# Attention and two expert layers on one core: two bursts of products with v per chunk instead of three, and the inverse sums spread by ScalarE

## The chip, the core and the metric

The kernel runs on one core of a Trainium2 chip. The metric is the device time of one execution in microseconds. Three executions of the kernel before took 1208.04, 1212.86 and 1212.77 us, median 1212.77. Five engines work side by side: TensorE (PE, its weight loads PEld), VectorE (DVE), ScalarE (ACT), GpSimd (POOL) and the DMA queue of SyncE (SP). They meet only at semaphores.

## The reference, cut to what matters

```python
q_rot, k_rot = rotate(q), rotate(k)              # 2 batches, 8 heads, 576 positions, 64 wide
scores = matmul(q_rot, k_rot.T) / sqrt(64)
attn = exp(scores - scores.max(-1))
attn = attn / (attn.sum(-1) + 1e-9)
x = matmul(attn, v)                              # then 1152 x 512
x = (silu(x @ w_gate) * (x @ w_val)) @ w_out     # 512 -> 1536 -> 512
P = sinkhorn(exp(x @ w_gate2 - max))             # 8 rounds, 8 experts
out = sum_e P[:, e] * (relu(x @ w1[e]) @ w2[e])  # 512 -> 1024 -> 512
```

The change is in the attention alone, in the sums, their inverses and the product with v.

## The kernel before

The 16 heads are taken as 8 pairs, numbered n = 0 to 7. A pair has nine units u = 0 to 8. Each is a tile of 128 queries by 576 keys, and unit 4 holds the last 64 queries of both heads. For a unit TensorE makes the scores `s` (L257), VectorE takes the negative row maximum `ng` (L262), ScalarE takes the exponential `p` and adds up the row sums as it goes (L278), and TensorE turns `p` around by four transposes into `t` (L297), which VectorE, or ScalarE for units 0, 2 and 6, copies to SBUF (L312, `turned`). Eight of the nine units leave 64 columns over; they are turned together (`rest`, L319 to L323) and copied into `q` by VectorE (L328).

The product with v is made per chunk. Chunk 0 covers units 0 to 3 (256 queries), chunk 1 units 4 to 8 (320 queries). Five products j = 0 to 4 (`values`, L364) add up in one PSUM tile `pv`; j = 0 to 3 read the turned `p`, j = 4 reads `q`. Each j is two matmuls, one for each head of the pair, that write the two halves of the partitions. In the trace each of these fp32 matmuls shows as two records, so a single j is four records, and one head's matmul is two.

The sums are inverted once per chunk (`inverse`): VectorE adds 1e-9 (L333), takes the reciprocal (L334), copies the four columns of it out to 64 columns each, `iv` (L336), and for chunk 1 two blocks of 64 x 64 into the tile `both` (L340). TensorE turns `iv` around and multiplies `both` by `fold` (L349, L351), ScalarE copies the outcome to `rc` (L355), and VectorE multiplies `pv` by `rc` (L373, `summed`), which gives the attention's output `xf`.

The work is set out in steps. Pair n starts at step 9n with unit 0; each step has slots in a fixed order (`SLOTS`: pe0 is the scores, act0 the exponentials, dve0 the copies of turned weights, dve1 the sums, dve2 the row maxima, pe1 the turning, pe2 the rest, pe3 the spreading and the products with v). Four tables place the chunk's work in steps after t0 = 9n + 5 (chunk 0) or 9n + 10 (chunk 1): `REST`, `SPREAD`, `VALUES` (one step for each j) and `SUMMED`.

```python
SPREAD = (0, 2)
VALUES = ((1, 1, 3, 4, 4), (1, 2, 2, 4, 4))
SUMMED = (7, 6)
```

TensorE and ScalarE are held to the slots' order within a step; VectorE's order is found by the scheduler, and then each engine runs its list strictly in order. PSUM is tight: two buffers for scores, two for `t` (turned weights and the spread sums share them) and two for `rest` and `pv`. So the scores of unit u + 2 wait for the exponential of unit u, and each third use of `t` waits for the copy of the first. GpSimd meanwhile prepares the next pairs' rotated q and k, and two half tiles of the first layer's weights are converted (L120 to L136) in the steps of pairs 2 and 3. The gated layer (`gated`) and the experts (`experts`) follow when the attention's last `xf` is there.

Of the kernel before, what the change touches and what calls it, by code (L numbers as in the profile page):

```python
# [10 lines left out]
F32 = mybir.dt.float32  # L11
F32R = mybir.dt.float32r
U32 = mybir.dt.uint32
AF = mybir.ActivationFunctionType
ALU = mybir.AluOpType
# [3 lines left out]
B, H, S, D = 2, 8, 576, 64  # L19
# [21 lines left out]
ENGINES1 = ("vvvv", "pppv")  # L41
LOAD_V = -2
REST = (1, 0)
SPREAD = (0, 2)
VALUES = ((1, 1, 3, 4, 4), (1, 2, 2, 4, 4))
SUMMED = (7, 6)
ACT_TURNS = (0, 2, 6)
CONVERSIONS = (18, 32)
WARM = 20
# [7 lines left out]
def fused(ctx, tc, qk, v, rope, wgv, wo, wg2, w1, w2, out):  # L57
    nc = tc.nc
# [94 lines left out]
    def attention(xT, W):  # L153
        with ExitStack() as st:
            inp.append(pool("inp", bufs=2, stack=st))
            ap_ = pool("att", stack=st)
# [14 lines left out]
            X, HL, ST, P, SUM, PT, PV, R, XF, RC, SC, TP = ({} for _ in range(12))  # L171
# [154 lines left out]
            def rested(n, c):  # L326
                ps = R.pop((n, c, "rest"))
                nc.vector.tensor_copy(out=parts(n, c)[1], in_=ps[:, 0:CS[c][1]])  # L328

            def inverse(n, c):  # L330

                s1 = SUM.pop((n, c))
                nc.vector.tensor_scalar(out=s1, in0=s1, scalar1=1e-9, scalar2=None, op0=ALU.add)  # L333
                nc.vector.reciprocal(out=s1, in_=s1)  # L334
                R[n, c, "inv"] = iv = ap_.tile([128, 4, D], F32, tag="iv", name="iv")
                nc.vector.tensor_copy(out=iv, in_=s1[:, 0:4].unsqueeze(2).to_broadcast([128, 4, D]))  # L336
                if c == 1:
                    for h in range(2):
                        r = slice(64 * h, 64 * h + 64)
                        nc.vector.tensor_copy(out=both[r, r], in_=s1[r, 4:5].to_broadcast([64, 64]))  # L340

            def spread(n, c, part):

# [42 lines left out]
            def at(step, slot, fn, *args):  # L386
                plan.setdefault((max(step, FIRST), SLOTS.index(slot)), []).append((fn, args))
# [5 lines left out]
            for n in range(pairs):  # L393
                b = 9 * n
                if n > 1:
                    at(max(b + LOADS[1], 2), "load", load, n, 1)
                    at(max(b + LOADS[0], 2), "load", load, n, 0)
                if n:
                    at(b + LOAD_V, "load", load_v, n)
                    t0, t1 = (b + TURNS[1], b + TURNS[0]) if n > 1 else (b + TURNS1[1], b + TURNS1[0])  # L400
                    for i, t in ((1, t0), (0, t1)):
                        w = LAG if n > 1 and i else 0

                        e0, e1, e2, e3 = ENGINES1[i] if n == 1 else "pppp" if i else "pppv"
                        for dt, e, fn, args in ((0, e0, mult, (0,)), (1 + w, e1, mult, (1,)), (2 + w, e2, add, ()),
                                                (3 + w, e3, low, ())):
                            if fn is low:
                                at(t + dt, "act1", high, n, i)
                            at(t + dt, *(("pool", fn, n, i, *args, pool_) if e == "p" else ("dve3", fn, n, i, *args, nc.vector)))
                        at(b + STACKS[i] if n > 1 else t + 3, "dma", stack, n, i, nc.sync)  # L410
                for u in range(9):
                    at(b + u, "pe0", scores, n, u)
                    at(b + u, "dve2", row_max, n, u)
                    at(b + u + 1, "act0", exps, n, u)
                    at(b + u + 2, "pe1", turn, n, u)
                    if u in ACT_TURNS:
                        at(b + u + 2, "act2", turned, n, u)
                    else:
                        at(b + u + 3, "dve0", turned, n, u)
                for c in range(2):  # L420
                    t0 = b + 5 + 5 * c
                    at(t0, "dve1", inverse, n, c)
                    at(t0 + REST[c], "pe2", rest, n, c)
                    at(t0 + REST[c] + 1, "dve1", rested, n, c)
                    at(t0 + SPREAD[c], "pe3", spread, n, c, 0)
                    at(t0 + SPREAD[c], "act3", spread, n, c, 1)
                    for j in range(5):
                        at(t0 + VALUES[c][j], "pe3", values, n, c, j)
                    last = n == pairs - 1
                    ts = t0 + SUMMED[c]  # L430
                    at(ts, "dve3", summed, n, c)
                    if last:
                        cs = slice(CS[c][0], sum(CS[c]))
                        at(ts, "pool", finish, n, 0, cs)
                        at(ts, "dma", finish, n, 1, cs, nc.vector)
                    elif c == 1:
                        at(ts + 1, "act1", finish, n, 0)
                        at(ts + 1, "pool", finish, n, 1, slice(0, S), pool_)
# [14 lines left out]
            for x in blocks:  # L453
                nc.gpsimd.memset(x.bitcast(F32), 0.0)
            both = ap_.tile([128, 128], F32, name="both")
            nc.gpsimd.memset(both, 0.0)
            fold = ap_.tile([128, 64], F32, name="fold")
            nc.gpsimd.tensor_tensor(out=fold, in0=ident[:, 0:64], in1=ident[:, 64:128], op=ALU.add)
            tab = tabs[1]
# [242 lines left out]
    xT = new_x()  # L702
    W = {}
    attention(xT, W)
    ps = pool("ps", bufs=8, space=PSUM)
    x2 = new_x()
# [59 lines left out]
```

## Time and profile before

| what | value |
|---|---|
| median of three executions | 1212.77 us |
| the profiled execution's own time | 1212.68 us |
| its span, first to last instruction | 1210.6 us |
| TensorE busy, weight loads, VectorE, ScalarE, GpSimd | 99%, 89%, 45%, 28%, 7% |
| first score product of pair 0 | 13.90 us |
| first product of the gated layer | 178.21 us |
| share of TensorE in the chain that ended last | 94% |

The span is cut into an attention of about 164 us and dense layers of about 1030 us, in which TensorE works without a break. A busy share over the whole span says little about the attention; the pairs have to be read one by one. A pair is cut here at the first score product of its unit 0.

### The profile page before, as it was taken

The page shows a single profiled execution, that of the slowest core. Times are in us where ns is not written, and L with a number is a line of the kernel's source. Part 1 is how long each engine was busy: PE and PEld are TensorE (multiplying, and loading weights), DVE is VectorE, ACT ScalarE, POOL GpSimd, SP SyncE. Part 2 cuts the span into 40 slices and gives each one's busy share as a digit, 9 for nine tenths or more (in the row PEclk, how much of TensorE's full clock was granted, in tenths as well). Part 3 has the DMA queues.
Part 4 walks back from the last instruction along what each step waited for, and adds up shares of the span by engine and source line. Part 5 has one row for each costly group of instructions (what it writes and reads, how often), then busy time and mean ns, then how long its engine had stood idle before and what let it go on. Part 6 is the DMA issues. An engine that isn't in the chain of part 4 may idle for free.

```text
span 1210.6 us, 15264 instructions
## 1 busy us (share of the span) xinstructions
PE 1193.5 (99%) x6456; PEld 1074.7 (89%) x6456; DVE 542.0 (45%) x850; ACT 334.7 (28%) x599; POOL 90.5 (7%) x86
## 2 busy tenths in 40 slices
PE   7999999999999999999999999999999999999998
PEld 6666669999999999899899999989989989998997
DVE  7699868998742453232232332332323233233221
ACT  4556544443411412121131221212202112122110
POOL 5468400000000000000000000000000000000000
PEclk7899999999999999999999999999999999999999
DMA  4767503332211301010120220210102012020001
GB/s 158 207 163 187 144 25 116 120 125 87 88 53 57 135 1 53 30 58 19 52 70 1 70 70 1 70 68 3 49 22 70 15 56 70 1 70 1 9 18 52
DMA packets 24115, 80.52 MB, mean 67 GB/s; under 512 B 4272, under 2 KB 4784, under 8 KB 21872
## 3 DMA queue, kind: packets, MB, share of 16 engines
q1 hardware_dynamic: 24048, 79.56, 21.2%
q8 instruction: 50, 0.82, 0.3%
q14 instruction: 17, 0.14, 0.0%
HBM read 64.80 MB, written 2.36 MB: 55 GB/s over the span
## 4 chain that ended last, share of the span: by engine, by line
PE 94%; DVE 4%; DMA 1%; ACT 1%; issue 0%; SPq 0%; DVEq 0%; ACTq 0%
PE p L148 11%; PE p L150 11%; PE p L149 11%; PE p L603 11%; PE p L604 11%; PE p L602 11%; PE s L257 4%; PE pv L364 3%; PE t L297 2%; PE po L150 2%; PE po L149 2%; PE po L148 2%; PE pg L150 2%; PE pg L148 2%; PE pv L150 2%; PE pg L149 2%
## 5 line engine op out<-in xcount | busy, mean ns | idle before, releaser
L148 PE MATMUL p<-xh,wh 128*128 128x384 f32 x768 | 257.7, 336 | 0.0
L150 PE MATMUL p<-xh,wl 128*128 128x384 f32 x768 | 256.8, 334 | 0.0
L149 PE MATMUL p<-xl,wh 128*128 128x384 f32 x768 | 256.7, 334 | 0.0
L604 PE MATMUL p<-wh,hl 128*128 128x512 f32 x576 | 224.4, 390 | 0.0
L603 PE MATMUL p<-wl,hh 128*128 128x512 f32 x576 | 224.4, 390 | 0.0
L602 PE MATMUL p<-wh,hh 128*128 128x512 f32 x576 | 224.0, 389 | 0.0
L591 ACT ACTIVATE hh<-p 128x384 fp32r<-128x384 f32 x192 | 94.2, 491 | 370.6 <-PE p L150 370.6
L592 DVE SCALAR_TENSOR_TENSOR hl<-p,hh 128x384 fp32r<-128x384 f32 x192 | 106.8, 556 | 188.7 <-ACT hh L591 188.6
L609 DVE SCALAR_TENSOR_TENSOR acc<-p,Pm,acc 128x512 f32<-128x512 f32 x63 | 47.3, 750 | 254.1 <-PE p L604 254.1
L148 PEld LDWEIGHTS p<-xh,wh 128*128 128x128 f32 x768 | 144.2, 188 | 0.9
L149 PEld LDWEIGHTS p<-xl,wh 128*128 128x128 f32 x768 | 144.2, 188 | 0.6
L150 PEld LDWEIGHTS p<-xh,wl 128*128 128x128 f32 x768 | 144.1, 188 | 0.0
L99 ACT CAST wh<-raw 128x1024 fp32r<-128x1024 f32 x64 | 67.2, 1053 | 249.3 <-PE p L604 197.7
L604 PEld LDWEIGHTS p<-wh,hl 128*128 128x128 f32 x576 | 108.1, 188 | 22.5
L603 PEld LDWEIGHTS p<-wl,hh 128*128 128x128 f32 x576 | 108.1, 188 | 22.2
L602 PEld LDWEIGHTS p<-wh,hh 128*128 128x128 f32 x576 | 108.1, 188 | 22.1
L66 DVE TENSOR_TENSOR wl<-raw,wh 128x1024 fp32r<-128x1024 f32 x64 | 78.2, 1224 | 78.4 <-ACT wh L99 76.5
L262 DVE TENSOR_REDUCE ng<-s 128x1 f32<-128x576 f32 x72 | 53.5, 749 | 15.6 <-PE s L257 10.6
L278 ACT ACTIVATE p<-s,ng 128x576 f32<-128x576 f32 x64 | 47.6, 743 | 40.1 <-DVE ng L262 39.8
L148 PE MATMUL pg<-xh,wh 128*128 128x384 f32 x144 | 48.9, 339 | 3.1 <-ACT wh L129 2.4
L149 PE MATMUL pg<-xl,wh 128*128 128x384 f32 x144 | 48.5, 337 | 0.0
L150 PE MATMUL pg<-xh,wl 128*128 128x384 f32 x144 | 48.5, 337 | 0.0
(126 smaller groups left out, 1400.6 us busy)
## 6 DMA issues: line engine op xcount, KB each, us to landing
raw<-in_w SPq DMA_DIRECT2D x64, 512.0 KB, 3.9
raw<-in_wgv SPq DMA_DIRECT2D x11, 1024.0 KB, 4.9
x<-in_qk SPq DMA_DIRECT2D x15, 576.0 KB, 4.6
raw<-in_wo SPq DMA_DIRECT2D x6, 1024.0 KB, 4.9
x<-hl SPq DMA_DIRECT2D x42, 144.0 KB, 3.4
x<-hl SPq DMA_DIRECT2D x14, 288.0 KB, 3.3
v<-in_v SPq DMA_DIRECT2D x8, 320.0 KB, 5.0
out<-acc SPq DMA_DIRECT2D x9, 256.0 KB, 2.0
```

The lines of the kernel that those rows point to most:

```text
L66: (eng or nc.vector).tensor_tensor(out=out_, in0=a, in1=hi.bitcast(F32), op=ALU.subtract)
L99: nc.scalar.copy(out=hi, in_=raw)
L148: nc.tensor.matmul(ps, wh[wsl], xh[xsl], start=first, stop=False)
L149: nc.tensor.matmul(ps, wh[wsl], xl[xsl], start=False, stop=False)
L150: nc.tensor.matmul(ps, wl[wsl], xh[xsl], start=False, stop=last)
L257: nc.tensor.matmul(ps[:, c, o:o + ks.stop - ks.start], q, k, start=t == 0, stop=t == len(terms) - 1)
L262: nc.vector.tensor_reduce(out=R[n, u], in_=SC[n, u][:, :, 0:288], axis=AX.XY, op=ALU.max, negate=True)
L591: nc.scalar.activation(out=hh[:, f], in_=po, func=AF.Relu)
L592: nc.vector.scalar_tensor_tensor(out=hl[:, f], in0=po, scalar=0.0, in1=hh[:, f].bitcast(F32), op0=ALU.max, op1=ALU.subtract)
L602: nc.tensor.matmul(po, hh[:, f, tl], wh[:, ws], start=f == 0, stop=False)
L603: nc.tensor.matmul(po, hh[:, f, tl], wl[:, ws], start=False, stop=False)
L604: nc.tensor.matmul(po, hl[:, f, tl], wh[:, ws], start=False, stop=f == KF2 - 1)
```

## The change: what it does

```diff
-SPREAD = (0, 2)
-VALUES = ((1, 1, 3, 4, 4), (1, 2, 2, 4, 4))
-SUMMED = (7, 6)
+SPREAD = (1, 2)
+VALUES = ((2, 2, 4, 4, 4), (2, 2, 4, 4, 4))
+SUMMED = (5, 5)
...
+            def guard(n, c):
+                s1 = SUM[n, c]
+                nc.scalar.activation(out=s1, in_=s1, func=AF.Copy, bias=1e-9)
+
             def inverse(n, c):
 
+                s1 = SUM[n, c]
+                nc.vector.reciprocal(out=s1, in_=s1)
+
+            def along(n, c):
+
                 s1 = SUM.pop((n, c))
-                nc.vector.tensor_scalar(out=s1, in0=s1, scalar1=1e-9, scalar2=None, op0=ALU.add)
-                nc.vector.reciprocal(out=s1, in_=s1)
                 R[n, c, "inv"] = iv = ap_.tile([128, 4, D], F32, tag="iv", name="iv")
-                nc.vector.tensor_copy(out=iv, in_=s1[:, 0:4].unsqueeze(2).to_broadcast([128, 4, D]))
+                nc.scalar.copy(out=iv, in_=s1[:, 0:4].unsqueeze(2).to_broadcast([128, 4, D]))
                 if c == 1:
-                    for h in range(2):
-                        r = slice(64 * h, 64 * h + 64)
-                        nc.vector.tensor_copy(out=both[r, r], in_=s1[r, 4:5].to_broadcast([64, 64]))
+                    nc.scalar.activation(out=both, in_=mask, func=AF.Copy, scale=s1[:, 4:5])
...
+                    at(t0 - 1, "act1", guard, n, c)
                     at(t0, "dve1", inverse, n, c)
+                    at(t0, "act2", along, n, c)
...
-            nc.gpsimd.memset(both, 0.0)
+            mask = ap_.tile([128, 128], F32, name="mask")
+            nc.gpsimd.memset(mask, 0.0)
+            for h in range(2):
+                nc.gpsimd.memset(mask[64 * h:64 * h + 64, 64 * h:64 * h + 64], 1.0)
```

Each chunk's products with v stand in two steps instead of three: j = 0 and 1 at t0 + 2, the other three at t0 + 4. The multiplication by `rc` is two steps (chunk 0) or one step (chunk 1) earlier in the plan. VectorE keeps the reciprocal alone; ScalarE adds the 1e-9, copies `iv`, and fills `both` in one instruction from a mask of ones in its two diagonal blocks. `mask` is set once at the start, on GpSimd.

The first place is on TensorE, where chunk 1 of pair 5 begins, during units 2 and 3 of pair 6 (`pv` the products with v, `t` what is turned or spread; the numbers behind names are buffers). Before:

```order
L257 MATMUL s<-x_1505,x_1644 128x288 x4
L297 MATMUL t<-ident,p 128x128 x4
L364 MATMUL pv<-p_1722,v 64x320
L257 MATMUL s<-x_1508,x_1648 128x288 x4
L364 MATMUL pv<-p_1722,v 64x320
L297 MATMUL t<-ident,p 128x128 x4
L349 MATMUL t<-ident,iv 128x128 x2
L351 MATMUL t<-fold,both 128x64
L364 MATMUL pv<-p_1722,v 64x320 x4
```

And now, the same place:

```order
L257 MATMUL s<-x_1502,x_1641 128x288 x4
L297 MATMUL t<-ident,p 128x128 x4
L257 MATMUL s<-x_1505,x_1645 128x288 x4
L297 MATMUL t<-ident,p 128x128 x4
L354 MATMUL t<-ident,iv 128x128 x2
L356 MATMUL t<-fold,both 128x64
L369 MATMUL pv<-p_1716,v 64x320 x4
```

Before, the first j of this chunk stood as two single matmuls, one head on each side of a score product; now two whole j stand together behind the spread sums, and the step ahead of them has no product with v at all. The list before has such a divided j in chunk 1 of pairs 0, 1, 2, 4, 5 and 7, which five times is a place in the pair after it (pairs 1, 2, 3, 5 and 6); the changed list has none.

The second place is on TensorE, units 6 to 8 of pair 5, where chunk 0's first products are. Before:

```order
L257 MATMUL s<-x_1242,x_1388 128x288 x4
L297 MATMUL t<-ident,pL 128x128 x4
L321 MATMUL rest<-ident,p 128x128 x2
L257 MATMUL s<-x_1239,x_1384 128x288 x4
L364 MATMUL pv<-p_1591,v 64x256 x4
L297 MATMUL t<-ident,p 128x128 x4
L257 MATMUL s<-x_1242,x_1388 128x288 x4
L297 MATMUL t<-ident,p 128x128 x4
```

And now:

```order
L257 MATMUL s<-x_1240,x_1386 128x288 x4
L297 MATMUL t<-ident,pL 128x128 x4
L321 MATMUL rest<-ident,p 128x128 x2
L354 MATMUL t<-ident,iv 128x128 x2
L257 MATMUL s<-x_1237,x_1382 128x288 x4
L297 MATMUL t<-ident,p 128x128 x4
L369 MATMUL pv<-p_1588,v 64x256 x4
L257 MATMUL s<-x_1240,x_1386 128x288 x4
L297 MATMUL t<-ident,p 128x128 x4
```

The spreading of `iv` for chunk 0 has come down behind `rest`; the two transposing groups of units 4 and 5 now stand nearer to each other, with one score product between them and the products with v behind the second; and the lone j = 2 of the step after is gone.

The third place is on ScalarE, from unit 6 of pair 4 to unit 2 of pair 5 (`p_1464` before is `p_1459` now, the turned weights of chunk 1). Before:

```order
L312 COPY p_1464<-t 128x4x128
L278 ACTIVATE p,sum<-s,ng 128x576 x3
L312 COPY p_1591<-t 128x4x128
L278 ACTIVATE p,sum<-s,ng 128x576
L209 CAST hl_1524<-x 128x576
L278 ACTIVATE p,sum<-s,ng 128x576
L355 COPY rc<-t 128x320
```

And now:

```order
L312 COPY p_1459<-t 128x4x128
L278 ACTIVATE p,sum<-s,ng 128x576
L332 ACTIVATE sum<-sum 128x5
L278 ACTIVATE p,sum<-s,ng 128x576
L343 COPY iv<-sum 128x256
L345 ACTIVATE both<-mask,sum 128x128
L278 ACTIVATE p,sum<-s,ng 128x576
L312 COPY p_1588<-t 128x4x128
L209 CAST hl_1522<-x 128x576
L278 ACTIVATE p,sum<-s,ng 128x576
L360 COPY rc<-t 128x320
```

The addition to the sum stands behind the last exponential of chunk 1, and `iv` and `both` between the exponentials of the next pair's units 0 and 1.

## Rows read from the trace of the kernel before

**Rows 1.** Windows from pair to pair; per engine busy us (instructions), PE clock, DMA share, GB/s.

```profile
13.90:40.53 26.63, 25.59 (x110) 19.57 (x110) 17.38 (x27) 10.74 (x25) 13.24 (x12) 0.55 0.63 170
40.53:58.79 18.26, 18.26 (x129) 12.81 (x127) 14.75 (x28) 11.38 (x27) 8.13 (x8) 1.00 0.68 184
58.79:78.83 20.04, 18.81 (x129) 12.82 (x127) 19.06 (x33) 11.41 (x28) 12.82 (x11) 1.00 0.60 158
78.83:98.59 19.76, 18.64 (x129) 12.77 (x127) 18.42 (x33) 11.60 (x28) 14.32 (x13) 1.00 0.72 199
98.59:116.02 17.43, 17.43 (x127) 12.63 (x127) 15.43 (x31) 12.20 (x28) 12.68 (x11) 1.00 0.69 182
116.02:134.81 18.79, 18.29 (x128) 12.77 (x126) 15.88 (x28) 11.80 (x28) 13.71 (x12) 1.00 0.60 153
134.81:153.06 18.25, 18.25 (x128) 12.80 (x126) 14.93 (x28) 10.55 (x26) 4.63 (x6) 1.00 0.45 108
153.06:178.21 25.15, 24.47 (x173) 16.19 (x171) 17.04 (x38) 11.93 (x30) 2.34 (x2) 1.00 0.00 1
```

**Rows 2.** Chain that ended last, window 58.79 to 78.83, its shares by line.

```profile
by line: DVE ng L262 26.5%; DVE p L312 15.4%; DVE sum L333 13.6%; DVE raw L132 7.7%; issue 4.8%; ACT p L278 4.1%; DVE hl L66 3.8%; PE s L257 3.7%; DVE q L328 3.6%; DVE xf L373 3.6%; DVE cv L126 3.0%; ACT xh L379 2.8%; DVE cv L123 1.7%; DVE 
```

**Rows 3.** Timeline of TensorE, pair 6: start, us, engine, line, operation, tiles, count.

```profile
139.70 0.75 PE L364 MATMUL pv<-p,v 128*64 128x320 f32 x2
140.38 0.79 PE L257 MATMUL s<-x,x 128*128 128x288 f32 x4
```

**Rows 4.** Timeline of TensorE, pair 4.

```profile
102.97 0.60 PE L297 MATMUL t<-ident,p 128*128 128x128 f32 x4
103.51 0.76 PE L364 MATMUL pv<-p,v 128*64 128x320 f32 x4
104.19 0.80 PE L257 MATMUL s<-x,x 128*128 128x288 f32 x4
104.83 0.60 PE L297 MATMUL t<-ident,p 128*128 128x128 f32 x4
105.27 0.38 PE L349 MATMUL t<-ident,iv 128*128 128x128 f32 x2
...
105.75 1.30 PE L364 MATMUL pv<-p,v 128*64 128x320 f32 x8
106.98 1.06 PE L257 MATMUL s<-hl,bd 128*128 128x288 f32 x6
```

**Rows 5.** Groups by line, 13.90 to 178.21: busy us, mean ns, idle before.

```profile
L312 DVE COPY p<-t 128x512 f32<-128x512 f32 x48 | 32.8, 683 | 6.4 <-PE t L297 6.2
...
L278 ACT ACTIVATION_READ_ACCUMULATOR p<-s,ng 128x1 f32 x64 | 12.5, 196 | 0.0
...
L333 DVE TENSOR_SCALAR sum<-sum 128x4 f32<-128x4 f32 (+1 forms) x16 | 8.8, 549 | 1.9 <-ACT p L278 1.9
...
L355 ACT COPY rc<-t 128x256 f32<-128x256 f32 (+1 forms) x16 | 6.4, 399 | 9.7 <-PE t L349 4.8 <-PE t L351 4.7
...
L336 DVE COPY iv<-sum 128x256 f32<-128x256 f32 x16 | 6.2, 386 | 0.4
...
L340 DVE COPY both<-sum 64x64 f32<-64x64 f32 x16 | 5.4, 337 | 0.1
...
L123 DVE TENSOR_SCALAR cv<-cv 128x512 uint32<-128x512 uint32 x2 | 2.3, 1170 | 0.0
```

**Rows 6.** Timeline of GpSimd and VectorE at 60.9.

```profile
60.94 1.42 POOL L203 TENSOR_TENSOR x<-x 128x576 f32<-128x576 f32 x1
60.96 1.43 DVE L333 TENSOR_SCALAR sum<-sum 128x5 f32<-128x5 f32 x1
```

**Rows 7.** Timeline of all engines at 100.9.

```profile
100.92 0.81 PE L257 MATMUL s<-x,x 128*128 128x288 f32 x4
...
101.76 0.76 DVE L262 TENSOR_REDUCE ng<-s 128x1 f32<-128x576 f32 x1 [0.17 <-PE s L257]
...
102.55 0.74 ACT L278 ACTIVATE p<-s,ng 128x576 f32<-128x576 f32 x1 [0.58 <-DVE ng L262]
```

## Prediction

> **What bounds the kernel now.** I first cut the trace at the first score product of each pair and read the windows from pair to pair [rows 1]. From pair 1 on the granted clock is 1.00 (2.4 GHz), and the pairs still take different times: 18.26, 20.04, 19.76, 17.43, 18.79 and 18.25 us for pairs 1 to 6. In pairs 1, 4 and 6 TensorE is busy for the whole window: it bounds them. In pairs 2 and 3 it is not (18.81 of 20.04, 18.64 of 19.76), VectorE is at 19.06 and 18.42 us, and the chain of waits of pair 2 is almost all VectorE, with 13.6% in L333, an addition to five numbers per partition [rows 2]. Pair 5 lies between. Pair 0 runs at half clock (0.55 in the mean). Everything after 178.21 us is dense TensorE work that the change doesn't touch; it starts when the last `xf` is there. So what the attention saves should come off the end, us for us.
>
> Why do two pairs that TensorE bounds differ by 0.82 us (18.25 for pair 6, 17.43 for pair 4)? The timeline of TensorE tells. In pair 6 chunk 1's first j is divided: one head's matmul takes 0.68 us to the next score product, and the other head's stands behind that [rows 3]. In pair 4 both heads' matmuls together take 0.68 us [rows 4]: they run side by side, and a divided j pays for it twice. The division is in pairs 1, 2, 3, 5 and 6, as the order before has it, and not in pair 4.
>
> **The change, part by part.** The sum is against the profiled execution, 1212.68 us, which is 0.09 under the median of 1212.77.
>
> *The divided products.* The new order has none. In pairs 1, 5 and 6 that is 3 x 0.82 = 2.5 us. In pairs 2 and 3, which VectorE sets, it is counted below with the rest.
>
> *One burst less per chunk.* What a burst costs by itself: a single j took 0.68 us from start to start, two j together 1.23, so a second burst costs 2 x 0.68 - 1.23 = 0.13; turning four blocks took 0.54 us to the next start when a burst follows and 0.44 when other 128-wide work follows, 0.10 more [rows 4]. That is 0.23 us, and two chunks make 0.46 us a pair: a pair that TensorE bounds would fall from 17.43 to 16.97.
>
> *What then comes late.* The saved time is taken from two short steps, units 1 and 2, which now have no products at all, and there other waits are close. From the start of a score product to its row maximum it is 0.84 us, another 0.79 to the exponential, 0.74 for that [rows 7]; the scores two units on need its buffer, some 0.1 later, so two steps can't be shorter than about 2.5 us. Unit 1 stays as it was: unit 2's scores began 0.64 us, a score product's time to the next start, ahead of the turning at 102.97 [rows 4], so at 102.33, 1.41 after unit 1's. Unit 2 is now a score product and a turning, 0.64 + 0.44 = 1.08. Together 2.49: the limit is just reached. And unit 5's turning now stands one score product behind unit 4's instead of behind the products as well. It needs the `t` buffer of unit 4, which VectorE frees with a copy of 0.68 us [rows 5] that comes after unit 6's row maximum: 0.84 + 0.75 + 0.68 = 2.3 us after unit 6's scores began. TensorE needs two score products (1.28), a turning (0.44) and, by the 0.48 that `iv` and `fold` take in pair 4 [rows 4], under 0.5 for `rest` and `iv`: 2.1 to 2.2. I give back 0.25 us a pair for both (bounds: 0, and all 0.46). So 17.2 us for a pair bound by TensorE. Pairs 1, 4, 5 and 6 sum to 72.73 before and 68.8 after: -3.9 us, the divided products and 0.54 us of VectorE's lag in pair 5 among it.
>
> *VectorE's relief.* L333, L336 and L340 go: 8.8 + 6.2 + 5.4 = 20.4 us over 8 pairs, 2.5 us a pair [rows 5], far more than such small operations need, since they wait for GpSimd: the L333 at 60.96 lasts 1.43 us, and ends with GpSimd's L203 that began just before it [rows 6]. Where TensorE bounds, this is worth nothing by itself. In pairs 2 and 3 it takes VectorE from 19.06 and 18.42 to about 16.5 and 15.9 us, below TensorE's 17.2. All of it would give 2 x 17.2, that is 5.4 us; but both pairs carry a conversion, five operations of which L123 takes 1.17 us [rows 5], and these come in one cluster between units 2 and 6, where unit 3's copy and the `t` buffers wait behind them. From 17.2 (all waits gone) to 19.9 (none gone) I take 18.5 for each, about the middle, as VectorE's saving is real but the cluster stays: 39.80 to 37.0, -2.8 us.
>
> *ScalarE's new work.* The trace has none of its three operations. The addition lies between nothing and 0.4 us; the nearest row is the accumulator's read, 0.20 on one column. `iv` is 256 wide, as half the `rc` copies are, mean 0.40 [rows 5]. For `both`, 128 wide with a scale per partition, I take 0.3; the lower end is the 0.20 of a one-column read, the upper the 1.43 of the longest L333, if ScalarE too had to wait for GpSimd. Per pair 2 x (0.20 + 0.40) + 0.3 = 1.5 us, on an engine with 10.6 to 12.2 us busy of 17 to 18. It stands idle before the exponentials, 0.58 us for one, waiting for a row maximum [rows 7]. The reciprocal that `iv` needs stands on VectorE ahead of that same row maximum, so the wait for it ends first. I cost it at nothing; if that cover is gone it costs up to 1.5 us a pair.
> The Trainium skill's page "SBUF — State Buffer" (SBUF: two separate sides) says that VectorE and GpSimd share a pair of ports as an exclusive lock and that ScalarE never waits on anyone. The trace agrees on VectorE (1.43 us, to the end of L203); by the rule the upper end of 1.43 us for `both` falls away and the 0.3 stays; no run so far shows it.
>
> *The ends.* Pair 0 loses one burst behind its unit 8 (0.23 at full clock, twice that at half): -0.4. Pair 7 and the tail lose two bursts and a divided j that partly lay under a copy: -0.5.
>
> Sum: -3.9 - 2.8 - 0.4 - 0.5 = -7.6, so 1212.7 - 7.6 = 1205 us.
>
> **Rivals.**
> 1. *The short steps eat the bursts, and the conversions' cluster keeps pairs 2 and 3.* For it: the 2.49 against 2.5 us above, and 0.1 to 0.2 us lacking at unit 5; VectorE's order is strict, so a lag of one operation reaches the next `t` buffer. Against: pair 4 runs without a wait while VectorE has 15.43 us. Then only the divided products are won, 3 x 0.82 in pairs 1, 5, 6 and some 0.8 each in 2 and 3, 4.1 us with nothing at the ends: 1208.6.
> 2. *VectorE's relief counts in full.* Pairs 2 and 3 at 17.2 (-5.4 instead of -2.8) and half of the 0.25 given back (4 x 0.12): 1205 - 2.6 - 0.5 = 1202.
> 3. *The clock rises later.* The first window's mean clock of 0.55 [rows 1] means 1.2 GHz for some 24 of its 26.6 us, with TensorE busy for 25.59 of them, and 2.4 GHz from about 38 us on. The way of `iv` now crosses ScalarE; if TensorE has to stop for it in that window and the half speed lasts half as long again, 12 us, these do 6 us less work: 1205 + 6 = 1211, no change. Against: at half clock TensorE is the slow one, and the other engines are ahead of it.
> 4. *Slower: ScalarE stands in its own way.* It runs strictly in order. If `iv` waits for a reciprocal that VectorE reaches late, the next unit's exponential waits behind it, then the scores two units on, then all of TensorE. Price: the added 1.5 us a pair on the path, 8 x 1.5 = 12, less the 5 us of the divided products with the tail's: 1212.7 + 7 = 1219.7. It decides from the point where the wait and the 0.7 us of `iv` and `both` outlast ScalarE's idle time ahead of the next exponential, which is 0.58 us in the place of [rows 7]. Against: the reciprocal comes first in VectorE's order, and ScalarE idles in each pair for 5 to 8 us [rows 1].
> [...]
>
> That the change doesn't do what it says is ruled out for the bursts by the order; it can be true of the relief, if VectorE's next operation waits for GpSimd in place of the removed one. That is within case 1.
>
> **How the numbers follow.** Chances: the forecast (1203.5 to 1207.5) 0.48; rival 1 (1207.5 to 1210) 0.20; rival 2 (under 1203.5) 0.20; rival 3 0.06; rival 4 and anything else slower 0.06. About 0.5%, 6.1 us, is what a measurement of this kernel can tell from no change; its three executions lie 0.4% apart. Faster is so under 1206.6. Rival 2 lies there whole, and of the forecast's four microseconds the lower three, some 0.8 of it: 0.8 x 0.48 + 0.20 = 0.58. Slower is 0.06, and no change the rest, 0.36. The range for 8 in 10 holds the forecast and most of rivals 1 and 2: 1200 to 1210.
>
> **What would show it.** Right: windows of about 17.2 us for pairs 1, 4, 5, 6, equal among themselves; no two-record product of v around a score product; L333 and L340 gone from the chain; pairs 2 and 3 at 18 to 19 us with VectorE still near full; ScalarE's idle time before exponentials shorter by about 1.5 us a pair. The turning of unit 5 would show a short wait for a copy by VectorE. Wrong: waits of TensorE for the exponentials behind `iv`; pair 4 above 17.43; a clock of 0.5 beyond 40 us; or the attention shorter and the gated layer's first wait for weights longer by as much.

## The result and the profile after

Six executions of the changed kernel took 1199.15 to 1200.43 us, median 1199.96. Six of the kernel before took 1206.41 to 1212.86, median 1207.94. The ratio is 0.9916, with a 95% interval of 0.9894 to 0.9938: faster by 8.0 us. I had forecast 1205.0 with a range from 1200 to 1210, so the time came out at the lower edge, 0.04 us outside. The forecast gain of 7.6 us was close. What failed is the level from which it was subtracted, and that is mainly the clock in pair 0, as the rest shows.

The profiled execution took 1199.97 us, span 1198.2. Its windows from pair to pair, with the columns of [rows 1]:

```profile
13.96:34.59 20.63, 19.19 (x107) 15.58 (x107) 15.96 (x25) 10.67 (x26) 11.69 (x11) 0.72 0.53 135
34.59:51.76 17.17, 17.13 (x129) 12.80 (x127) 12.46 (x23) 12.23 (x31) 9.17 (x10) 1.00 1.00 285
51.76:70.36 18.60, 17.58 (x129) 12.77 (x128) 16.56 (x28) 13.11 (x33) 12.71 (x11) 1.00 0.65 181
70.36:89.23 18.87, 17.40 (x130) 12.83 (x128) 16.61 (x27) 12.93 (x33) 13.49 (x12) 1.00 0.72 203
89.23:106.46 17.23, 17.18 (x126) 12.79 (x127) 13.23 (x24) 12.63 (x32) 14.77 (x14) 1.00 0.70 192
...
140.87:165.42 24.55, 23.84 (x178) 16.69 (x176) 16.02 (x29) 14.31 (x38) 1.42 (x2) 1.00 0.00 1
```

Pairs 1, 4, 5 and 6 now take 17.2 us each (17.17, 17.23, 17.19 and 17.22), equal among themselves; together 68.8 us, the sum that was forecast. Pairs 2 and 3 together fell from 39.80 to 37.47, pair 7 by 0.60. The large difference is in the first row: pair 0 fell from 26.63 to 20.63, with a mean clock of 0.72 instead of 0.55. The stretch after the attention is nearly the same, 1032.8 us against 1032.4. Of the 12.7 us between the two profiled executions, 6.0 lie in pair 0 and 6.8 in pairs 1 to 7.

The chain of waits in pair 2 (51.76 to 70.36), its shares by line:

```profile
by line: DVE ng L262 14.6%; issue 12.7%; DMA x<-hl 10.3%; DVE p L312 9.7%; SPq L237 8.7%; POOL hl L66 7.6%; DVE cv L122 6.6%; PE pv L369 5.5%; PE t L297 4.7%; DVE hl L66 4.0%; PE s L257 3.9%; DVE cv L126 3.5%; DVE raw L132 3.2%; DVE xf L378
```

The addition to the sums, 13.6% in [rows 2], is gone, and what remains of VectorE there is mostly row maxima, copies and the conversion (L122, L126, L132); the first 5 us of the chain now run through the next pair's operands (POOL hl L66, SPq L237, DMA x<-hl). The groups from 13.96 to 165.42 that answer to [rows 5] (line, engine, operation, count, busy us, mean ns, idle before):

```profile
L343 ACT COPY iv<-sum 128x256 f32<-128x256 f32 x16 | 6.4, 398 | 0.3 <-DVE sum L337 0.3
...
L332 ACT ACTIVATE sum<-sum 128x4 f32<-128x4 f32 (+1 forms) x16 | 3.3, 208 | 0.4
L345 ACT ACTIVATE both<-mask,sum 128x128 f32<-128x128 f32 x8 | 3.2, 401 | 0.0
...
L123 DVE TENSOR_SCALAR cv<-cv 128x512 uint32<-128x512 uint32 x2 | 3.0, 1524 | 0.1
```

ScalarE's three operations take 0.21, 0.40 and 0.40 us, where VectorE's took 0.55, 0.39 and twice 0.34 on average, and up to 1.43 for one. The conversion's L123 has grown from 1.17 to 1.52.

The place of [rows 3, 4], TensorE in pair 6 after the change (start, us, line, operation, tiles, records):

```profile
126.39 0.80 PE L257 MATMUL s<-x,x 128*128 128x288 f32 x4
...
128.91 0.81 PE L257 MATMUL s<-x,x 128*128 128x288 f32 x4
129.55 0.60 PE L297 MATMUL t<-ident,p 128*128 128x128 f32 x4
...
130.50 1.30 PE L369 MATMUL pv<-p,v 128*64 128x320 f32 x8
131.72 1.06 PE L257 MATMUL s<-hl,bd 128*128 128x288 f32 x6
```

No half j stands around a score product any more; the eight records of two j take 1.22 us to the next start. Units 1 and 3 start 2.52 us apart, at the limit of 2.5 that the prediction worked out, and TensorE has no wait there.

### The profile page after: what moved, and what is told of

The parts are those of the page before. It is cut to its first block, busy times and chain, and to the rows that moved or that the text cites. A ratio compares the mean times of both kernels' runs of the same rounds, so it can differ in the third digit from the quotient of the medians.

```text
span 1198.2 us, 15270 instructions
## 1 busy us (share of the span) xinstructions
PE 1179.4 (98%) x6456; PEld 1070.6 (89%) x6456; DVE 525.5 (44%) x802; ACT 342.7 (29%) x639; POOL 89.9 (8%) x88
## 4 chain that ended last, share of the span: by engine, by line
PE 93%; DVE 3%; DMA 1%; issue 1%; ACT 1%; SPq 0%; POOL 0%; DVEq 0%; POOLq 0%
PE p L148 11%; PE p L150 11%; PE p L149 11%; PE p L614 11%; PE p L613 11%; PE p L612 11%; PE s L257 3%; PE pv L369 3%; PE t L297 2%; PE po L150 2%; PE po L149 2%; PE po L148 2%; PE pg L150 2%; PE pg L148 2%; PE pv L150 2%; PE pg L149 2%
## 5 line engine op out<-in xcount | busy, mean ns | idle before, releaser
L66 DVE TENSOR_TENSOR wl<-raw,wh 128x1024 fp32r<-128x1024 f32 x64 | 78.1, 1223 | 78.4 <-ACT wh L99 76.5
L262 DVE TENSOR_REDUCE ng<-s 128x1 f32<-128x576 f32 x72 | 54.0, 753 | 19.2 <-PE s L257 17.2
```

What stands on the lines that cost most here:

```text
L66: (eng or nc.vector).tensor_tensor(out=out_, in0=a, in1=hi.bitcast(F32), op=ALU.subtract)
L262: nc.vector.tensor_reduce(out=R[n, u], in_=SC[n, u][:, :, 0:288], axis=AX.XY, op=ALU.max, negate=True)
```

## Experiments

Theory A throughout: in pairs 1 to 7 the change works as forecast, and what differed is when TensorE's clock rises in pair 0, which is not of the change's making. Theory B: the change itself shortened pair 0, or one of its parts is worth something other than I said.

### The same kernels again

`e1_before_again` is the kernel before, unchanged, and `e5_after_again` the changed one, unchanged.

> The kernel before, unchanged, to see its executions one by one. Theory A (the clock's rise in pair 0 varies from execution to execution, whatever the kernel): the executions fall into two groups about 5 us apart, near 1207.5 and near 1212.5, and a profile of the faster kind has pair 0 at about 21 us with the clock up near 25 us, pairs 1 to 6 as in the profile shown (18.3, 20.0, 19.8, 17.4, 18.8, 18.3 within 0.3). Theory B (the change brings the earlier rise): every execution near 1212.5, or, if faster, with the clock still rising near 38 us.

Measured: 1211.54 us median of 12 executions, 1205.51 to 1213.08, ratio to the others beside it 0.9998 (0.9976 to 1.0020). Five executions were at 1205.5 to 1207.8 and seven at 1210.8 to 1213.1. The profile fell on the slower kind: the clock rose at 38.55 us, and pair 0 took 28.04. So the kernel before was not seen in a trace with an early rise; that it has one is read from its mean clocks below.

> The changed kernel once more, beside many executions of before on the same chip, for the clock in pair 0. Theory A (when the clock rises to 2.4 GHz in pair 0 is left to the execution): its executions spread as those of before do, over some 5 us, from about 1199 to 1205, and beside an equal clock the gain is 6.5 to 8 us. Theory B (the change itself brings the early rise): all executions stay within 1199 to 1200.5.

Measured: 1200.99 median of 12, 1197.87 to 1208.50, ratio 0.9937 (0.9913 to 0.9961). Both kernels spread over some 10 us, in groups by the mean clock of the execution. Put side by side at an equal clock (90 executions of the kernel before that ran beside the experiments, 18 of the changed one; the table has the clocks that both show):

| mean granted clock | before, mean us (count) | after, mean us (count) | difference |
|---|---|---|---|
| 0.987 | 1213.22 (13) | 1205.54 (1) | -7.7 |
| 0.988 | 1212.39 (9) | 1205.17 (1) | -7.2 |
| 0.991 | 1209.26 (1) | 1201.71 (2) | -7.6 |
| 0.992 | 1207.80 (24) | 1200.36 (6) | -7.4 |
| 0.993 | 1207.79 (3) | 1199.99 (5) | -7.8 |
| 0.994 | 1205.86 (13) | 1198.51 (2) | -7.4 |

At an equal clock the change is worth 7.2 to 7.8 us. Most of the remaining spread is pair 0. Windows of the changed kernel there, from its first profile:

```profile
14.00:26.00 12.00, 10.96 (x48) 9.12 (x48) 10.18 (x15) 5.73 (x14) 4.52 (x5) 0.52 0.39 112
26.00:38.00 12.00, 11.60 (x84) 8.75 (x84) 8.13 (x15) 8.04 (x21) 8.72 (x8) 1.00 0.80 190
```

And of `e4_conversions_late` below, which has the same instructions on every engine in that stretch:

```profile
14.00:26.00 12.00, 10.96 (x48) 9.07 (x48) 10.19 (x14) 5.73 (x14) 4.68 (x6) 0.50 0.39 113
26.00:38.00 12.00, 12.00 (x47) 8.94 (x47) 5.58 (x10) 5.15 (x12) 8.06 (x7) 0.50 0.82 198
```

The first 12 us are alike. In the next 12 one execution runs at 2.4 GHz (clock 1.00) and the other at 1.2, with 84 matmul records against 47. So the same work sees the rise at 26 or at 38 us, and 12 us at half speed are 6 us of work. Between the profiled executions of before and after it was the same: 38.01 against 25.60.

The change alone does not decide it. An early rise also stands in the traces of `e2_tables_only` and `e9_three_undivided` below (26.27 and 25.29 us), which keep VectorE's old work, and a late one in those of `e4_conversions_late` and `e11_addition_on_vectore` (38.47 and 38.18), of which the first has the whole change and the second all of it but the move of the addition.

Pair 0 is not the only place. In the profile of `e5_after_again` the clock rose early (25.33) but fell once more, from 90.18 to 93.59 us, behind stops of TensorE of 1.04 and 0.70 us at the end of pair 3. The windows of its pairs 3 and 4:

```profile
70.22:89.75 19.53, 17.47 (x130) 12.83 (x127) 16.79 (x27) 13.04 (x33) 13.42 (x12) 1.00 0.70 196
89.75:108.55 18.80, 18.76 (x127) 13.61 (x127) 13.26 (x24) 12.64 (x32) 14.74 (x14) 0.91 0.64 176
```

So pairs 1 to 7 of this execution of the changed kernel sum to 133.09 us, not 130.83. In the first profile stops of 0.78 and 0.69 us at the same place brought no fall. A mean clock does not tell where in an execution the half clock lay.

### The two parts of the change alone

`e2_tables_only` is the kernel before with the three tables alone:

```diff
-SPREAD = (0, 2)
-VALUES = ((1, 1, 3, 4, 4), (1, 2, 2, 4, 4))
-SUMMED = (7, 6)
+SPREAD = (1, 2)
+VALUES = ((2, 2, 4, 4, 4), (2, 2, 4, 4, 4))
+SUMMED = (5, 5)
```

> The three tables alone: two bursts per chunk and no divided j, VectorE keeps the addition and the spreading copies. My account: pairs 1, 4, 5, 6 at 17.2 to 17.5 us, pairs 2 and 3 still near 19.5 to 20 as VectorE keeps its 2.5 us a pair; about 1203 us with an early clock (0.4% under before). Rival: the short units need VectorE's relief to hold, every pair is at 17.8 us or more, and the time is 1205 to 1207.

Measured: 1213.59 us (1209.97 to 1219.90), ratio 1.0033 (1.0009 to 1.0058): slower, by 0.1 to 2.5 us at an equal clock. Pairs 1 to 7 sum to 142.40 us, 4.7 more than before, and TensorE waits 1.3 to 1.5 us at unit 3 in each of pairs 4 to 6. In pair 3 it stops for 3.06 us, and 3.4 us of half clock follow (80.89 to 84.30), so some of the 4.7 us is the clock:

```profile
72.64:96.14 23.50, 19.02 (x129) 14.14 (x127) 21.00 (x33) 11.87 (x28) 14.10 (x13) 0.93 0.58 163
```

The rival's mechanism held, every pair at 17.80 us or more; its time was too low. The place in pair 6, from all engines:

```profile
136.37 1.42 POOL L203 TENSOR_TENSOR x<-x 128x576 f32<-128x576 f32 x1
136.58 1.36 DVE L336 COPY iv<-sum 128x256 f32<-128x256 f32 x1
...
138.62 0.75 DVE L262 TENSOR_REDUCE ng<-s 128x1 f32<-128x576 f32 x1
...
139.40 0.74 ACT L278 ACTIVATE p<-s,ng 128x576 f32<-128x576 f32 x1 [3.29 <-DVE ng L262]
...
140.28 0.79 PE L257 MATMUL s<-x,x 128*128 128x288 f32 x4 [1.30 <-ACT p L278]
```

Read from the end: the scores wait 1.30 us for an exponential, that for a row maximum, and the row maximum stands in VectorE's list behind the copy of `iv`, which lasts as long as GpSimd's L203 beside it. In the two short steps the old way of spreading the sums no longer has cover.

`e3_scalar_only` is the changed kernel with `VALUES` and `SUMMED` as before; it keeps the later spreading of chunk 0:

```diff
-VALUES = ((2, 2, 4, 4, 4), (2, 2, 4, 4, 4))
-SUMMED = (5, 5)
+VALUES = ((1, 1, 3, 4, 4), (1, 2, 2, 4, 4))
+SUMMED = (7, 6)
```

> ScalarE's part alone (and the spreading one step later in chunk 0, which it needs), products with v in three bursts as before; the order now divides a j only in pair 1 and at the tail. My account: pair 1 at 18.25, pairs 4, 5, 6 at 17.4, pairs 2 and 3 at 18 to 18.6; 1203 us with an early clock. Rival (ScalarE's added 1.5 us a pair costs): pairs 4 to 6 at 17.8 or more and 1206 to 1208.

Measured: 1200.73 us (1199.12 to 1205.41), ratio 0.9932 (0.9908 to 0.9956). Its windows of pairs 1, 2 and 4 (pair 3 took 17.96):

```profile
38.52:56.78 18.26, 18.26 (x129) 12.81 (x127) 12.91 (x22) 12.48 (x32) 8.17 (x9) 1.00 0.81 220
56.78:74.56 17.78, 17.66 (x129) 12.61 (x127) 16.31 (x27) 13.35 (x34) 12.21 (x11) 1.00 0.69 183
...
92.52:109.97 17.45, 17.45 (x127) 12.66 (x127) 13.70 (x24) 13.23 (x34) 13.54 (x12) 1.00 0.67 185
```

Pairs 1 to 7 sum to 131.51, 6.16 less than before; at an equal clock it took 6.2 to 7.1 us less. The order of this version divides a j only for the place in pair 1 (18.26) and at the end; pairs 4 to 6 stand at 17.43 to 17.45. Which of its two differences made the scheduler drop the other divisions was not tested. So ScalarE's part, with the later spreading, brings 6.16 of the 6.84 us of pairs 1 to 7, and the tables 0.68 on top of it: -1.1 in pair 1, -0.2 in each of pairs 4 to 6, -0.65 in pair 7, and +0.8 and +0.9 in pairs 2 and 3, where the conversions are.

`e9_three_undivided` is the kernel before with the first three of chunk 1's products later by a step, still in three steps, which keeps each j whole:

```diff
-VALUES = ((1, 1, 3, 4, 4), (1, 2, 2, 4, 4))
+VALUES = ((1, 1, 3, 4, 4), (2, 3, 3, 4, 4))
```

> The kernel before with one number of a table changed: chunk 1's products with v at steps 2, 3, 3, 4, 4 after t0 instead of 1, 2, 2, 4, 4, so still three bursts and VectorE's work untouched, but in the order no j is divided. Theory (a divided j costs 0.82 us wherever TensorE bounds): pairs 1 and 6 fall from 18.25 to 17.4, pair 5 to 18.0, pairs 2 and 3 stay at 19.2 to 20 as VectorE sets them; at an equal clock 2.5 to 3.5 us less than before. Rival: the division was only a sign of TensorE waiting there, and the pairs stay at 18.2.

Measured: 1211.34 us (1209.18 to 1216.51), ratio 1.0031 (1.0012 to 1.0050): slower, by 1.9 to 3.4 us at an equal clock. TensorE's busy time does fall (in pair 5 from 18.29 to 17.70), but waits take its place: that pair still takes 18.61, and pair 4, which had no divided j before, rises from 17.43 to 18.35. In pair 6:

```profile
134.57 1.42 POOL L203 TENSOR_TENSOR x<-x 128x576 f32<-128x576 f32 x1
134.60 1.42 DVE L333 TENSOR_SCALAR sum<-sum 128x5 f32<-128x5 f32 x1
...
136.36 0.71 DVE L262 TENSOR_REDUCE ng<-s 128x1 f32<-128x576 f32 x1
...
137.10 0.74 ACT L278 ACTIVATE p<-s,ng 128x576 f32<-128x576 f32 x1 [2.15 <-DVE ng L262]
...
137.99 0.79 PE L257 MATMUL s<-x,x 128*128 128x288 f32 x4 [0.60 <-ACT p L278]
```

Pairs 1 and 6 stay at 18.06 and 18.36. The row maximum stands behind an addition that lasts as long as GpSimd's L203, and with no product in that step TensorE waits for it. The run takes the division away only by moving the products, so it does not tell what a whole j in its old place would bring; pair 4 before, which has one there, took 17.43.

`e11_addition_on_vectore` is the changed kernel with the addition back on VectorE, `iv` and `both` still on ScalarE:

```diff
+                nc.vector.tensor_scalar(out=s1, in0=s1, scalar1=1e-9, scalar2=None, op0=ALU.add)
...
-                    at(t0 - 1, "act1", guard, n, c)
```

> The changed kernel with the addition of 1e-9 back on VectorE, in front of the reciprocal; the two spreading copies stay on ScalarE, TensorE's order is unchanged. Theory: the addition's long waits for GpSimd (8.8 us over the 16 chunks) are in pairs where GpSimd works: pairs 2, 3 and 5 rise by 0.5 to 1.5 us, pairs 6 and 7 hardly; 1.5 to 3 us more than the changed kernel at an equal clock. Rival: the addition is hidden, as in the pairs that TensorE bounds, and the time is the changed kernel's within 0.5 us.

Measured: 1204.94 us (1199.43 to 1209.41), ratio 0.9952 (0.9930 to 0.9974). In its profile the clock rose at 38.18, and 6 of its 10 executions had a mean clock of 0.988 or less. At 0.992 it took 1199.43 and 1199.89, the changed kernel 1200.36 in the mean; pairs 1 to 7 sum to 131.02 against 130.83. On VectorE the addition takes 0.43 us in the mean, and it is hidden. The rival holds: with the copies on ScalarE it does not matter where the addition stands. What is left for the gain of `e3_scalar_only` is the move of the two spreading copies.

### The conversions

What keeps pairs 2 and 3 at 18.6 and 18.9? The prediction said: the cluster of conversion operations. VectorE, ScalarE and TensorE of the changed kernel in pair 3:

```profile
84.21 1.51 DVE L126 SCALAR_TENSOR_TENSOR cv<-raw,cv 128x512 uint32<-128x512 uint32 x1
...
85.64 0.75 DVE L262 TENSOR_REDUCE ng<-s 128x1 f32<-128x576 f32 x1
...
86.42 0.74 ACT L278 ACTIVATE p<-s,ng 128x576 f32<-128x576 f32 x1 [1.62 <-DVE ng L262]
...
87.30 0.80 PE L257 MATMUL s<-x,x 128*128 128x288 f32 x4 [0.78 <-ACT p L278]
```

The row maximum stands behind an L126 of 1.51 us, and through the exponential TensorE waits 0.78. Are these operations slow by themselves, or because of GpSimd? `e4_conversions_late` moves the conversions to steps 54 and 62, so into pair 6 and on into pair 7, in which GpSimd has less to do:

```diff
-CONVERSIONS = (18, 32)
+CONVERSIONS = (54, 62)
```

> The changed kernel with the two conversions of half a weight tile moved from the steps of pairs 2 and 3 to those of pairs 6 and 7. Theory: the conversions' cluster on VectorE is what keeps pairs 2 and 3 at 18.6 and 18.9 us against 17.2: they fall to 17.2, a gain of 3.0 us, and pairs 6 and 7 rise by less than that, since GpSimd is nearly idle there and VectorE's operations don't wait for it: 1197 to 1198.5 us. Rival (something else of pairs 2 and 3, such as GpSimd's own work on the next pairs, keeps them): they stay above 18.3, pairs 6 and 7 rise, and the time is 1200 or more.

Measured: 1207.77 us (1206.77 to 1212.91), ratio 0.9995 (0.9978 to 1.0012). Pairs 2 and 3 fell to 17.22, as the theory had it, but pair 6 took 26.30:

```profile
143.53 1.27 POOL L136 TENSOR_TENSOR wl<-cv,raw 128x512 fp32r<-128x512 f32 x1
...
144.82 0.33 SPq L114 DMA_DIRECT2D raw<-in_wgv  x1
...
145.25 0.46 SPq L231 DMA_DIRECT2D x<-hl  x1
...
152.12 1.30 PE L257 MATMUL s<-x,x 128*128 128x288 f32 x4 [8.27 <-DMA x<-hl]
```

The second conversion's load (L114) needs the buffer that the first one's last operation (L136) frees, and on SP's queue the transfers for pair 7's operands (L231) stand behind it. TensorE waits 8.27 us and the clock is at 0.50 from 147.7 to 157.9. Pair 7 took 27.20. The operations were cheap there (L122, L123 and L126 of the second conversion took 0.43, 0.43 and 0.69 us), but 8 steps between the two conversions are too few.

`e10_conversions_54_68` keeps them 14 steps apart, as in the original:

```diff
-CONVERSIONS = (18, 32)
+CONVERSIONS = (54, 68)
```

> The changed kernel with the two conversions at steps 54 and 68, 14 apart, where GpSimd has next to no work of its own; TensorE's order is unchanged. Theory (what the conversions cost pairs 2 and 3 is VectorE's operations waiting for GpSimd): pairs 2 to 5 at 17.2, pairs 6 and 7 up by 0.3 each, so 2.5 us less than the changed kernel at an equal clock, 1195.4 for its fastest executions. Rival (the five operations cost pairs 6 and 7 as much, or the last conversion ends after the attention and the gated layer waits): no less than 1198 for the fastest.

Measured: 1197.06 us (1196.02 to 1207.90), ratio 0.9923 (0.9890 to 0.9955). Pairs 1 to 7 sum to 128.81 us, 2.0 less than the changed kernel, where 2.5 was expected: pairs 2 and 3 fell to 17.22, but pairs 6 and 7 rose by 0.58 and 0.40. Its windows of pairs 2 and 6 (pair 3 reads as pair 2):

```profile
51.53:68.75 17.22, 17.18 (x130) 12.80 (x127) 12.71 (x23) 12.18 (x31) 11.75 (x11) 1.00 0.70 192
...
120.41:138.21 17.80, 17.36 (x130) 12.79 (x127) 14.91 (x28) 12.46 (x32) 7.44 (x8) 1.00 0.50 119
```

And VectorE in the first conversion there, with GpSimd idle from 127.77 to 132.55 us:

```profile
128.25 0.41 DVE L122 TENSOR_SCALAR cv<-cv 128x512 f32<-128x512 f32 x1
...
128.70 0.43 DVE L123 TENSOR_SCALAR cv<-cv 128x512 uint32<-128x512 uint32 x1
...
129.24 0.68 DVE L126 SCALAR_TENSOR_TENSOR cv<-raw,cv 128x512 uint32<-128x512 uint32 x1
```

The same operations beside a busy GpSimd, in pair 2 of the changed kernel:

```profile
59.20 2.97 POOL L199 TENSOR_TENSOR x<-x,tab 128x576 f32<-128x576 f32 x2
...
59.61 1.29 DVE L122 TENSOR_SCALAR cv<-cv 128x512 f32<-128x512 f32 x1
...
60.93 1.53 DVE L123 TENSOR_SCALAR cv<-cv 128x512 uint32<-128x512 uint32 x1
```

0.84 us for L122 and L123 together against 2.82. The cluster costs what it does because of GpSimd, and at an equal clock this version beats both kernels: at 0.994 it took 1196.55 in the mean of four executions, the changed kernel 1198.51 in the mean of two.

### A longer warm-up

20 matmuls of ones keep TensorE busy until 7.75 us; then it idles to 13.96, and the clock falls at 11.95. `e6_before_warm44` and `e7_after_warm44` change this in the kernel before and in the changed one:

```diff
-WARM = 20
+WARM = 44
```

> The kernel before with 44 warm-up matmuls on TensorE at its start instead of 20, so that it has no idle stretch of 5 us ahead of its first scores (they end at 13 to 14 us instead of 7.4 to 8.8). Theory A: the clock stays at 2.4 GHz through pair 0, pair 0 falls from 26 to 28 us to under 20, the spread between executions goes, and the time is 1203 to 1205 us. Rival: other engines bound pair 0, it stays at 20 to 21 us with the clock high, and the time is about 1206 with little spread. If the clock falls all the same, nothing changes.

> The changed kernel with the same 44 warm-up matmuls. Theory A: both kernels now have the same clock throughout, so the difference to the kernel before with 44 is the change alone: pairs 1 to 7 by 6.2 us plus what pair 0 gives, 6.5 to 8 us, and 1196 to 1198 us. Theory B: the difference falls to under 5 us, as the early rise was part of the change's effect.

Measured: 1205.98 us (1205.40 to 1209.28, ratio 0.9978, 0.9956 to 1.0000) and 1199.27 us (1198.71 to 1200.11, ratio 0.9916, 0.9884 to 0.9948). The difference between the two is 6.7 us, so Theory B of the second falls. Their profiles have the same length of half clock in pair 0, 10.24 us, and the same stretch behind the attention, 1030.04: the span is 7.5 us shorter, 6.2 of it in pairs 1 to 7 and 1.35 in pair 0, which took 23.27 and 21.92 us. This is the change without the clock. The aim, a clock that stays up, was missed: VectorE's list now had the next pair's rotation ahead of the first row maxima, TensorE stopped for 3.83 us at 15.9, and the clock was at 1.2 GHz from 18.95 to 29.19 in the one and from 17.11 to 27.35 in the other.

`e8_after_warm44_conv` adds conversions at other steps to `e7_after_warm44`; the edit is shown against the changed kernel:

```diff
-CONVERSIONS = (18, 32)
-WARM = 20
+CONVERSIONS = (48, 62)
+WARM = 44
```

> The changed kernel with 44 warm-up matmuls and the two conversions at steps 48 and 62 instead of 18 and 32. In the run with steps 54 and 62 the second conversion's load waited on SyncE's queue for the first one's buffer, and pair 7's stacking transfers behind it; 14 steps apart, as in the kernel before, that wait should be gone. Theory: pairs 2 and 3 at 17.2 us, pairs 5 to 7 up by under 1 us each, 2 to 3 us less than without the move: 1194 to 1196 us. Rival: the load still stands in the queue ahead of the stacking transfers, a pair waits for them, and the time is that of the version without the move or more.

Measured: 1199.60 us (1198.81 to 1207.46), ratio 0.9932 (0.9909 to 0.9955). Pairs 2 and 3 took 17.22, but pair 5, with the first conversion, 19.78: GpSimd is still at work there, L123 took 1.53 us and L126 1.78, and TensorE waits 1.67 us at 122.81. The rival's time held, though not by the queue: at a clock of 0.995 this version took 1199.23 us in the mean, `e7_after_warm44` 1199.27. It is GpSimd's work and not the pair's number that sets the price.

`e12_warm_start` is the version of `e10_conversions_54_68` with the longer warm-up, and with VectorE held to the written order in the first two steps; the edit is shown against `e10_conversions_54_68`:

```diff
-WARM = 20
+WARM = 44
...
-                with tc.manual_schedule(engines=ORDERED - OUTER):
+                with tc.manual_schedule(engines=(START if step < 2 else ORDERED) - OUTER):
```

> The changed kernel with the conversions at steps 54 and 68, 44 warm-up matmuls ahead of the first score product, and VectorE held to the written order in the first two steps, so that only one multiplication for the next pair (about 1.5 us) stands ahead of the second unit's row maximum. Theory A (what the time of a run differs by is the clock in pair 0, and that falls where TensorE stops for long): with TensorE busy until its first score product and no stop above some 2 us behind it, the clock stays at 2.4 GHz, pair 0 takes under 20 us, and the time is 1190 to 1194 us with the executions within 3 us of each other. Rival: the stops that remain ahead of units 1 to 3 of pair 0 let the clock fall all the same; then pair 0 takes 21 to 24 us and the time is 1196 to 1198 us, what the version with the late conversions had at a clock of .994.

Measured: 1199.10 us (1196.69 to 1205.00, 4 executions), ratio 0.9886 (0.9853 to 0.9919). TensorE at the start of pair 0:

```profile
14.12 1.91 PE L257 MATMUL s<-hl,hl 64*128 64x288 f32 x15 [0.72 <-ACT hl L209]
17.64 1.06 PE L257 MATMUL s<-hl,hl 64*128 64x288 f32 x6 [1.61 <-ACT p L278]
...
21.85 2.37 PE L257 MATMUL s<-hl,hl 64*128 64x64 f32 x9 [2.57 <-ACT p L278]
```

The stops are 1.61 and 2.57 us instead of one of 3.83, and in the second, at 19.37, the clock falls all the same; in this profile it rose only at 46.68, and pair 0 took 28.09. Theory A's condition, no stop above some 2 us, was not met, so this run does not test it; the rival's mechanism holds, at a higher price in this profile than it had. At a clock of 0.996 two executions took 1196.69 and 1196.82, no better than the best of the version without warm-up, 1196.0: what the clock gave back did not show in the time. The low ratio comes from the seven executions of the kernel before beside it, median 1212.47, five of them at 0.989 or less; it is no gain over the others.

## Why the prediction was right or wrong

**The step that failed** is in *The ends*: "Pair 0 loses one burst behind its unit 8 ...: -0.4", together with the sum "against the profiled execution, 1212.68 us". I took that execution's pair 0, 26.63 us with a rise at 38.01, as a fixed property of the kernel. It is one draw of something that varies: the kernel before itself took 1205.1 to 1216.5 us in 90 executions. The profile showed the handle (0.55 in the first window of [rows 1]), and the three times before, 1208.04 beside 1212.86 and 1212.77, showed two levels; I used them only as a width for "no change". Rival 3 looked at the same window for a later rise alone; an earlier one, 12 us at twice the speed, so 6 us, belonged beside it with much the same chance, and the range had to reach to some 1198. Taking the change off a mean over such draws, about 1208 to 1211, gives 1200 to 1203. That the time lies only 0.04 us outside is luck of the draw. That the gain comes near 7.6 is not, since it is 7.2 to 7.8 at an equal clock, though two errors in it cancel: pairs 2 and 3 gave less than forecast, and the -0.4 was too small: with the rise at 38 us in both, pair 0 lost some 0.7 us (25.94 in the profile of `e11_addition_on_vectore` against 26.63), and 1.35 between the two kernels with the longer warm-up.

**Bursts and what comes late.** Forecast 17.2 us for a pair that TensorE bounds, measured 17.17 to 17.23. The net of -0.46 and +0.25 shows alone between `e3_scalar_only` and the changed kernel: 17.43 to 17.2, 0.21 to 0.24 a pair. The limit of 2.5 us for two short steps was met at 2.52, without a wait. Pair 7 gave 0.60 for the 0.5 forecast.

**The divided products.** The total of pairs 1, 4, 5 and 6, -3.9, came out exactly, but it hung on a condition that the prediction did not name. In the old tables both its prices hold. Pair 1 of `e3_scalar_only`, relieved but still divided, stays at 18.26, and pair 4, undivided before and there, goes from 17.43 to 17.45: the relief alone is worth nothing. Pair 6, which loses its division there, falls by 0.82. In the new order the relief is worth more than the nothing that I put down "where TensorE bounds": without it the two short steps lay VectorE's wait for GpSimd bare, and pairs 4 to 6 take 18.6 to 18.8 us (`e2_tables_only`), or 18.35 to 18.6 where the products of chunk 1 alone are moved (`e9_three_undivided`). That pair 4 ran without a wait beside a VectorE of 15.43 us did not carry over to a pair with shorter steps. Whether the divisions could have been avoided in their old place without the relief, no run shows.

**VectorE's relief.** For pairs 2 and 3 forecast -2.8, measured -2.33; the conversion's cluster stays as said, and `e10_conversions_54_68` shows what it holds back: without it both are 17.22, the end that rival 2 had worked out. That its price is GpSimd's work was not in the prediction.

**ScalarE's new work.** 0.21, 0.40 and 0.40 us against 0.20, 0.40 and 0.30; costed at nothing, and right. For chunk 1 of pair 6, which stands in pair 7's window, it fits between two exponentials (ScalarE alone):

```profile
142.50 0.21 ACT L332 ACTIVATE sum<-sum 128x5 f32<-128x5 f32 x1
142.61 0.72 ACT L278 ACTIVATE p<-s,ng 128x576 f32<-128x576 f32 x1
...
143.33 0.39 ACT L343 COPY iv<-sum 128x256 f32<-128x256 f32 x1
...
143.62 0.40 ACT L345 ACTIVATE both<-mask,sum 128x128 f32<-128x128 f32 x1
...
145.24 0.74 ACT L278 ACTIVATE p<-s,ng 128x576 f32<-128x576 f32 x1 [1.22 <-DVE ng L262]
```

ScalarE is done with both 1.22 us before the next row maximum is there, and pairs 4 to 6 of `e3_scalar_only` show no cost, so rival 4 did not come. All 16 copies of `iv` took 0.39 to 0.41 us and all 8 of `both` 0.40, GpSimd busy or not. The Trainium skill's page "SBUF — State Buffer" (SBUF: two separate sides) says that ScalarE never waits on anyone; the trace agrees for these copies. Its page "ScalarE: Activation LUTs" (Rules for kernel authors) sends additions to VectorE. Here the addition took 0.21 us on ScalarE and 0.43 in the mean on VectorE (`e11_addition_on_vectore`), with no difference in time. The copies made one: pairs 1 to 7 took 142.40 us with all three operations on VectorE (`e2_tables_only`, with 3.4 us of half clock in pair 3) and 130.83 with them on ScalarE; one copy on VectorE took 1.36 us beside GpSimd.

**What stays open.** Whether the change makes an early rise likelier. Of the 18 executions of the changed kernel 15 had a mean clock of 0.991 or more, of the 90 before 41. In `e5_after_again` it was 10 of 12, and 17 of 29 for the kernel before that ran beside it; of `e11_addition_on_vectore`, which differs by one small operation, 4 of 10. The runs show both rises with and without the change, but not what decides, and I did not find an experiment that fixes it: the three warm-up versions moved the fall and did not prevent it.

## What to carry to other kernels

Before a difference is subtracted from a time, ask whether that time is one draw: a first window at half clock, and times on two levels, mean that the forecast needs both levels, and that versions are compared at an equal clock. A step made shorter on one engine can lay bare a wait of another: here two steps without products cost more than they saved until VectorE's small operations, which waited for GpSimd, were gone. So ask of each part of a change what it is worth without the others. When a small operation lasts several times what its size needs, look for the engine that it waits for, and move it to one that doesn't.

## What was not expected of the hardware

With 20 warm-up matmuls the granted clock fell between 10.9 and 14.1 us, in TensorE's idle time ahead of the first score product or just behind it, and the pair-0 work then ran at 1.2 GHz until anywhere from 25.3 to 38.6 us, though TensorE was busy for 10.96 us of the 12 from 14 on in both cases shown above. VectorE's L122 and L123 took 0.41 and 0.43 us with GpSimd idle, 1.29 and 1.53 beside it; ScalarE's copies did not change. A stop of 8.27 us brought 10.2 us of half clock, from its middle on. And TensorE does have a break in the dense layers, other than said at the start: about 15 us into the gated layer it stops for the next weights, 2.44 us in the kernel before and 2.70 in the changed one. In both 3.4 us of half clock came with it (195.02 to 198.44, 182.61 to 186.03), and none with the 2.64 us there in `e10_conversions_54_68`.
